# Dense layer with GELU, forward and backward: another place for the 64 left-over columns, other first loads, and a regrouped turn from block 0 to block 1

## The chip, the core and the metric

The kernel runs on one core of a Trainium2 chip, in one launch. The metric is the device time of that launch in microseconds (us). The core has five engines that run side by side and meet through semaphores: TensorE (PE in the profile, with its weight loads as PEld), VectorE (DVE), ScalarE (ACT), GpSimd (POOL) and SyncE (SP), which only issues DMAs here. ACT and POOL can issue DMAs too; all DMAs share 16 DMA engines.

## What is computed

```python
# x: 2048 x 448, w1: 448 x 1792, w2: 1792 x 448, b1: 1792, b2: 448; all bf16
h   = gelu(x @ w1 + b1)        # tanh form of GELU
out = h @ w2 + b2
# returned: out, and for a given grad_out the gradients of x, w1, b1, w2, b2
```

With u = x @ w1 + b1 and gh = (grad_out @ w2^T) * gelu'(u), the gradients are gx = gh @ w1^T, gw1 = x^T @ gh, gb1 = the column sums of gh, gw2 = h^T @ grad_out and gb2 = the column sums of grad_out.

## The kernel before

**Sizes.** The inner dimension of 448 is three tiles of 128 (`KF` = 3) and 64 left-over columns (`DL` = 64). The 2048 rows are cut into four blocks of 512 (`NB`, `SB`). The 1792 hidden columns are 14 tiles, taken in seven pairs (`NPAIR`). A step `g` is one pair of one block, so there are 28 steps; block 0 is steps 0 to 6.

**One step.** For the pair, PE makes u with w1 as weights (`M1`, L226, three products of 512 columns for each half, six in all) and q = grad_out @ w2^T (`M4`, L245, six products). The 64 left-over columns of both are done by `rest`: one product of u uses the lower 64 rows of the array (L236) and one of q the upper 64 rows (L239), and the two run side by side. To make that fit, x lies so that its left-over columns are in partitions 0 to 63 of the fourth tile and grad_out has its own in partitions 64 to 127. ACT then adds the bias and copies u to V (`act_first`, L252, two), squares it (L253), takes the GELU (L254), and in `act_second` a tanh (L272). DVE forms the derivative: `dve_first` (Bt, L269), `dve_second` (p, then t+1, p-0.5 and their product: L276, L277, L278, L279) and `dve_gate`, which multiplies with q out of PSUM into ghT (L282).

**Products of the blocks.** A `Unit` is one row tile of `out` ("o") or `gx` ("g"): 14 products of 448 columns (L313), one for each hidden tile, spread over the steps by `seq` and `grow`. In block 0 each step does eight of them (four "o" units, two products each), which need the two w2 tiles of that step. A finished unit is moved out of PSUM by ACT (L327) or DVE (L329) in `flush`, and stored by POOL (L333).

**Buffers that tie the order.** q has one PSUM buffer, so `rest(g+1, g)` of the next step waits for `dve_gate` of the step before. u has one PSUM buffer, so `M1(g+2)` waits for ACT's two copies of `act_first(g+1)`. V, A and Bt have one buffer each.

**Order of a step.** The loop at the end of the main function writes the order out by hand: `rest(g+1, g)`, `M4(g)`, DVE's evictions, `dve_gate(g)`, `act_first(g+1)`, ACT's evictions, `dve_first(g+1)`, `act_second(g+1)`, `dve_second(g+1)`, the products of the units, `M1(g+2)`. In step 6 the products come ahead of `act_second`; in step 7 the first four products come ahead of `M1(9)` and the rest behind it.

**The start.** SP issues, one behind the other: x of block 0 as two transposing DMAs (three tiles, L139, then one tile, L140), grad_out as two (L144, L145), w2^T for the first pair as two (L155, L156), then w2, w1 and w2^T in pieces (L152, L148/L149, L155/L156), x and grad_out of block 1, and w1^T. ACT issues b1 (L171) and w1 columns 0 to 255; POOL clears six tiles of `gh_nat` (L168) and then issues w1 columns 256 to 511. PE starts with seven products of zeros (L180), the 14 one-column products that turn b1 into a column (L184), and three more products of zeros (L187). Before `M4(0)` it does four products whose result nobody reads (L384). I call all of these awake-products.

**The end.** After step 27, "o" and "g" units of the last block are finished, then gw1 (L471, L479) and gw2 (L490) are made from all rows.

Of the kernel before, what the change touches and what calls it, by code (L numbers as in the profile page):

```python
# [18 lines left out]
def kernel(  # L19
# [15 lines left out]
    nc = tc.nc  # L35
    P = 128
    B, S, D = x.shape
# [3 lines left out]
    NF = F // P  # L41
    KD = (D + P - 1) // P
    KF = KD - 1
    DL = D - KF * P
    DOV = D - P
    DM = KF * P
    SB = 512
    NB = S // SB
    SPB = SB // P
    NPAIR = NF // 2  # L50
# [3 lines left out]
    x2 = x.rearrange("b s d -> (b s) d")  # L54
# [26 lines left out]
    gh_nat = const.tile([P, NB, NF, SB], BF16, name="gh_nat")  # L81
# [7 lines left out]
    w1_sb = w1_flat.rearrange("p (k f) -> p k f", k=KD)  # L89
# [9 lines left out]
    def xq(b):  # L99
        o = (b % 2) * 2 * KD * SB  # L100
        return xg_flat[:, o:o + KD * SB].rearrange("p (k s) -> p k s", k=KD)

    def gq(b):
        o = ((b % 2) * 2 + 1) * KD * SB
        return xg_flat[:, o:o + KD * SB].rearrange("p (k s) -> p k s", k=KD)

    def ring(t, n, g):
        o = (g % n) * 2 * SB
        return t[:, o:o + 2 * SB].rearrange("p (h s) -> p h s", h=2)

    def hT(g):
        return ring(hT_flat, HR, g)

    def ghT(g):
        return ring(ghT_flat, GR, g)

    def V_of(g):
        return VA_flat[:, 0:2 * SB].rearrange("p (h s) -> p h s", h=2)

    def A_of(g):  # L120
        return VA_flat[:, 2 * SB:4 * SB].rearrange("p (h s) -> p h s", h=2)

    def B_of(g):
        return ring(B_flat, 1, g)

    def t_of(g):
        return ring(T_flat, 4, 2 * (g % 2))

    def p_of(g):
        return ring(T_flat, 4, 2 * (g % 2) + 1)  # L130
# [5 lines left out]

    def load_x(b):
        rows = slice(b * SB, (b + 1) * SB)
        nc.sync.dma_start_transpose(out=xq(b)[:, 0:KF, :], in_=x2[rows, DL:D])  # L139
        nc.sync.dma_start_transpose(out=xq(b)[:, KF, :], in_=x2[rows, 0:P])  # L140

    def load_g(b):
        rows = slice(b * SB, (b + 1) * SB)
# [1 line left out]
        nc.sync.dma_start_transpose(out=gq(b)[:, 0:KF, :], in_=g2[rows, 0:DM])  # L145

    def load_w1(eng, f0, f1):
        eng.dma_start(out=w1_sb[:, 0:KF, f0:f1], in_=w1[DL:D, f0:f1].rearrange("(k p) f -> p k f", p=P))  # L148
        eng.dma_start(out=w1_sb[0:DL, KF, f0:f1], in_=w1[0:DL, f0:f1])  # L149

    def load_w2(eng, t0, t1):
        eng.dma_start(out=w2_sb[:, t0:t1, :], in_=w2[t0 * P:t1 * P, :].rearrange("(t p) d -> p t d", p=P))  # L152

    def load_w2T(f0, f1):
        nc.sync.dma_start_transpose(out=w2T_sb[:, KF, f0:f1], in_=w2[f0:f1, DOV:D])  # L155
        nc.sync.dma_start_transpose(out=w2T_sb[:, 0:KF, f0:f1], in_=w2[f0:f1, 0:DM])  # L156
# [6 lines left out]
    b1_row = T_flat[0:1, 4 * SB:4 * SB + F]  # L163
# [1 line left out]
    nc.vector.memset(ones, 1.0)  # L165
    nc.vector.memset(w128[:], 1.0 / P)

    nc.gpsimd.memset(gh_nat[:, NB - 1, 0:6, :], 0.0)  # L168
    load_w1(nc.gpsimd, 256, 512)
    load_x(0)  # L170
    nc.scalar.dma_start(out=b1_row, in_=b1.rearrange("(o f) -> o f", o=1))  # L171
    load_w1(nc.scalar, 0, 256)
    nc.scalar.activation(out=T_flat[0:1, SB + 2:SB + 3], in_=ones, func=ACT.Gelu_apprx_tanh)
    load_g(0)
# [1 line left out]
    load_w2(nc.sync, 0, 2)  # L176
    load_w1(nc.sync, 512, 768)
    pw = psum_a.tile([P, SB], F32, name="acc")
    for i in range(7):
        nc.tensor.matmul(pw[:], lhsT=warm[:, 0:P], rhs=warm, start=True, stop=True)  # L180

    pb = psum_a.tile([P, SB], F32, name="acc")
# [3 lines left out]
    for i in range(3):  # L186
        nc.tensor.matmul(pw[:], lhsT=warm[:, 0:P], rhs=warm, start=True, stop=True)  # L187
    load_w2T(256, 512)
    load_w2(nc.sync, 2, 4)
    load_w1(nc.sync, 768, 1280)  # L190
    load_w2T(512, 768)
    load_w2(nc.sync, 4, 8)
    load_w2T(768, 1024)
    load_w1(nc.sync, 1280, F)
    load_w2T(1024, 1280)
    load_w2(nc.sync, 8, NF)
    load_w2T(1280, 1536)
    load_x(1)
    load_w2T(1536, F)
# [8 lines left out]
    def blk(g):  # L208
        return divmod(g, NPAIR)

    def cols(g, h):
        c = g % NPAIR
        return slice((2 * c + h) * P, (2 * c + h + 1) * P)
# [4 lines left out]
    def M1(g):  # L218
        if g == 0:
            u_of[g] = [psum_a.tile([P, SB], F32, name="acc")[:] for h in range(2)]  # L220
        else:
            u = psum_u.tile([P, 2, SB], F32, name="u")
            u_of[g] = [u[:, h, :] for h in range(2)]
        for h in range(2):
            for kt in range(KF):
                nc.tensor.matmul(u_of[g][h], lhsT=w1_sb[:, kt, cols(g, h)], rhs=xq(g // NPAIR)[:, kt, :],  # L226
                                 start=(kt == 0), stop=False, skip_group_check=True)
# [14 lines left out]
    def M4(g):  # L242
        for h in range(2):
            for kt in range(KF):
                nc.tensor.matmul(g_of[g][:, h, :], lhsT=w2T_sb[:, kt, cols(g, h)], rhs=gq(g // NPAIR)[:, kt, :],  # L245
                                 start=False, stop=(kt == KF - 1), skip_group_check=True)

    def act_first(g):
        u = u_of.pop(g)
        for h in range(2):  # L250
            ft = 2 * (g % NPAIR) + h
            nc.scalar.activation(out=V_of(g)[:, h, :], in_=u[h], func=ACT.Identity, bias=b1_col[:, ft:ft + 1])  # L252
        nc.scalar.activation(out=A_of(g), in_=V_of(g), func=ACT.Square, scale=math.sqrt(3.0 * GELU_C * GELU_A))  # L253
        nc.scalar.activation(out=hT(g), in_=V_of(g), func=ACT.Gelu_apprx_tanh)  # L254

# [12 lines left out]
    def dve_first(g):  # L268
        nc.vector.scalar_tensor_tensor(out=B_of(g), in0=A_of(g), scalar=3.0 * GELU_C, in1=V_of(g), op0=ALU.add, op1=ALU.mult)  # L269

    def act_second(g):
        nc.scalar.activation(out=t_of(g), in_=B_of(g), func=ACT.Tanh, scale=-1.0 / 3.0)  # L272


    def dve_second(g):
        nc.vector.scalar_tensor_tensor(out=p_of(g), in0=A_of(g), scalar=GELU_C, in1=hT(g), op0=ALU.add, op1=ALU.mult)  # L276
        nc.vector.tensor_scalar(out=t_of(g), in0=t_of(g), scalar1=1.0, scalar2=None, op0=ALU.add)  # L277
        nc.vector.tensor_scalar(out=p_of(g), in0=p_of(g), scalar1=-0.5, scalar2=None, op0=ALU.add)  # L278
        nc.vector.tensor_tensor(out=t_of(g), in0=t_of(g), in1=p_of(g), op=ALU.mult)  # L279

    def dve_gate(g):
        nc.vector.scalar_tensor_tensor(out=ghT(g), in0=t_of(g), scalar=1.0, in1=g_of.pop(g)[:], op0=ALU.add, op1=ALU.mult)  # L282

    def store_h(g):
        b, c = blk(g)
        nc.gpsimd.dma_start(out=hT_dram_v[:, 2 * c:2 * c + 2, b * SB:(b + 1) * SB], in_=hT(g))  # L286
# [50 lines left out]
    def run_pieces(units):  # L337
        for un in units:
            if un.piece():
                full.append(un)  # L340

    def flush(by_act=None):
        for un in [un for un in full if by_act in (None, un.by_act)]:
            full.remove(un)
            evict(un)
# [22 lines left out]
    rest(0, None)  # L368
    first_step(0)
    act_second(0)  # L370
    dve_second(0)
    M1(1)
    for g in range(NSTEP):
        b, c = blk(g)
        pieces = [U[k] for k in seq[b] for _ in range(NF)]
        n = len(pieces)
        own = pieces[n * c // NPAIR:n * (c + 1) // NPAIR]
        grown = [U[k] for k in grow[b] for _ in range(2)]
        nxt = g + 1 if g + 1 < NSTEP else None
        rest(nxt, g)  # L380
        if g == 0:

            for i in range(4):
                nc.tensor.matmul(pw[:], lhsT=w1_sb[:, 0, 0:P], rhs=xq(0)[:, 0, :], start=True, stop=True)  # L384
        M4(g)
        flush(False)
        dve_gate(g)
        if nxt is not None:
            act_first(nxt)
        flush(True)  # L390
        if nxt is not None:
            dve_first(nxt)
        last = b == 0 and c == NPAIR - 1
        if last:
            run_pieces(grown + own)
            flush(True)
        if nxt is not None:
            act_second(nxt)
            dve_second(nxt)
        if g == NPAIR:  # L400
            run_pieces(grown)
            M1(g + 2)
            run_pieces(own)
        elif not last:
            run_pieces(grown + own)
        if g != NPAIR and g + 2 < NSTEP:
            M1(g + 2)
        for _ in range(2):
            if g >= NPAIR - 1 and stored < g:
                store_h(stored)  # L410
                stored += 1
        if c == 2 and 0 < b < NB - 1:
            load_x(b + 1)
            load_g(b + 1)
        for t in turns.get(g, []):
            turn_gh(*t)
# [45 lines left out]
    for t0, t1 in ((0, 4), (4, HT)):  # L462
        n = (t1 - t0) * P
        for h in range(2):
            a0, a1 = t0 + h * HT, t1 + h * HT
            cs = slice(a0 * P, a1 * P)
            for kt in range(KF):
                ps = psum_a.tile([P, SB], F32, name="acc")
                psv = ps[:, 0:n].rearrange("p (t f) -> p t f", f=P)
                for st in range(NS):  # L470
                    nc.tensor.matmul(psv, lhsT=x_all[:, st, kt * P:(kt + 1) * P], rhs=gh_rows(st, a0, a1),  # L471
                                     start=(st == 0), stop=(st == NS - 1))
# [3 lines left out]
        for st in range(NS):  # L476
            for h in range(2):
                psv = ps[h * DL:(h + 1) * DL, 0:n].rearrange("p (t f) -> p t f", f=P)
                nc.tensor.matmul(psv, lhsT=x_all[:, st, KF * P:D], rhs=gh_rows(st, t0 + h * HT, t1 + h * HT),  # L479
                                 start=(st == 0), stop=(st == NS - 1), tile_position=(0, h * DL), skip_group_check=True)  # L480
        nc.scalar.copy(out=gw1_rem[:, t0 * P:t1 * P], in_=ps[:, 0:n])
        for h in range(2):
            nc.scalar.dma_start(out=out_2[KF * P:D, (t0 + h * HT) * P:(t1 + h * HT) * P],
                                in_=gw1_rem[h * DL:(h + 1) * DL, t0 * P:t1 * P])
# [45 lines left out]
```

## Time and profile before

| what | value |
|---|---|
| time of three runs | 275.56, 275.80, 275.88 us; median 275.8 us |
| the profiled execution, its own time | 275.59 us |
| its span, first to last instruction | 273.8 us |
| block 0, first `rest` of step 0 to first of step 7 | 10.46 to 45.34 us |
| blocks 1 to 3 (steps 7 to 27) | 45.34 to about 161 us |
| last units, gw1, gw2 | about 161 to 271 us |

The time of a run is a little longer than the span, which leaves out what lies before the first and after the last instruction. Times inside the profile count from the start of the span. A line of the timeline has the start, the length, the engine, the line of the kernel and the operation; in brackets stands how long the engine had been idle before it and what ended the wait. A letter q behind an engine's name marks its sequencer; DMA issues stand there, and their length is the time of the issue, not of the transfer.

### The profile page before, as it was taken

What the parts mean: (1) busy time and instruction counts of PE and PEld (TensorE: products, weight loads), DVE (VectorE), ACT (ScalarE), POOL (GpSimd) and SP (SyncE); (2) the same over time, 40 slices, a digit from 0 to 9 for tenths busy, and PEclk for the clock granted to TensorE, in tenths of its full rate; (3) what the DMA queues carried; (4) which work ended last, traced back from release to release, by engine and by line L of the source; (5) the groups of instructions that cost most, each with busy time, mean ns of one, the idle gap of its engine ahead of it and who ended that gap; (6) DMA issues with size and microseconds to landing.
All of it is one profiled execution on the core that took longest, in us unless ns stands there. A gap on an engine that the chain in (4) does not pass through costs nothing.

```text
span 273.8 us, 3596 instructions
## 1 busy us (share of the span) xinstructions
PE 267.6 (98%) x1406; PEld 123.7 (45%) x1406; DVE 189.3 (69%) x218; ACT 143.7 (52%) x188; POOL 54.6 (20%) x57
## 2 busy tenths in 40 slices
PE   7899999999999999999999999999999999999995
PEld 3343434443444344444444445554445655555552
DVE  0799999999999999999888871139999970000000
ACT  2878879788888778887777740011111221112111
POOL 6000002730301403033031135111700019400000
PEclk9999999999999999999999999999999999999999
DMA  7878979999999928055534339999999931101111
GB/s 164 172 190 193 213 117 170 274 317 246 199 242 203 249 58 163 24 154 122 138 113 79 110 105 217 325 335 241 165 201 273 225 100 57 44 9 50 50 51 35
DMA packets 101379, 43.78 MB, mean 160 GB/s; under 512 B 90353, under 2 KB 97905, under 8 KB 101362
## 3 DMA queue, kind: packets, MB, share of 16 engines
q1 hardware_dynamic: 94272, 26.68, 51.6%
q0 software_dynamic: 4544, 14.92, 16.9%
q10 hardware_dynamic: 2546, 1.95, 2.5%
q8 instruction: 11, 0.18, 0.3%
q14 instruction: 6, 0.05, 0.1%
HBM read 7.00 MB, written 14.23 MB: 78 GB/s over the span
## 4 chain that ended last, share of the span: by engine, by line
PE 82%; DVE 12%; ACT 2%; DMA 2%; issue 1%; DVEq 0%
PE acc L313 27%; PE acc L490 16%; PE acc L471 13%; PE q L245 10%; PE u L226 9%; PE u L236 4%; DVE Bt L269 3%; DVE T L276 3%; DVE ghT_h L282 3%; PE acc L479 2%; DMA xg_h<-in_x_dram 2%; DVE T L279 2%; DVE T L277 1%; DVE T L278 1%; ACT VA L252 1%
## 5 line engine op out<-in xcount | busy, mean ns | idle before, releaser
L313 PE MATMUL acc<-w_gw,hT_h 128*128 128x448 bf16 x224 | 46.3, 352 | 0.2 <-ACT VA L252 0.2
L313 PE MATMUL acc<-w1T_gw,ghT_h 128*128 128x448 bf16 x224 | 45.1, 352 | 0.0
L245 PE MATMUL q<-xg_h,w2T_g 128*128 128x512 bf16 x168 | 41.1, 381 | 0.0
L252 ACT ACTIVATE VA<-u,b_col 128x512 f32<-128x512 f32 x54 | 34.0, 679 | 13.5 <-PE u L236 12.9
L226 PE MATMUL u<-xg_h,w_x 128*128 128x512 bf16 x162 | 39.4, 379 | 0.8 <-DMA w_x<-in_w_dram 0.4
L282 DVE SCALAR_TENSOR_TENSOR ghT_h<-T,q 128x1024 bf16<-128x1024 bf16 x28 | 34.2, 1221 | 8.4 <-PE q L245 7.0
L272 ACT ACTIVATE T<-Bt 128x1024 bf16<-128x1024 f32 x28 | 29.6, 1056 | 13.9 <-DVE Bt L269 13.8
L471 PE MATMUL acc<-gh_nat,w_x 128*128 128x512 bf16 (+1 forms) x192 | 36.7, 353 | 0.0
L276 DVE SCALAR_TENSOR_TENSOR T<-VA,hT_h 128x1024 bf16<-128x1024 f32 x28 | 34.1, 1219 | 0.2 <-ACT hT_h L266 0.2
L269 DVE SCALAR_TENSOR_TENSOR Bt<-VA 128x1024 f32<-128x1024 f32 x27 | 32.9, 1219 | 0.0
L313 PEld LDWEIGHTS <-hT_h 128*128 128x128 bf16 x224 | 21.9, 98 | 22.0 <-issue 0.5
L313 PEld LDWEIGHTS <-ghT_h 128*128 128x128 bf16 x224 | 21.9, 98 | 20.9
L456 DVE TENSOR_TENSOR VA<-VA,gh_nat 128x1792 f32<-128x1792 f32 x14 | 30.0, 2142 | 0.5
L253 ACT ACTIVATE VA<-VA 128x1024 f32<-128x1024 f32 x27 | 28.5, 1057 | 0.9
L254 ACT ACTIVATE hT_h<-VA 128x1024 bf16<-128x1024 f32 x27 | 28.1, 1040 | 0.0
L471 PEld LDWEIGHTS <-w_x 128*128 128x128 bf16 x192 | 18.7, 98 | 17.8 <-issue 0.4
L245 PEld LDWEIGHTS <-w2T_g 128*128 128x128 bf16 x168 | 14.2, 97 | 24.9 <-issue 11.4
L226 PEld LDWEIGHTS <-w_x 128*128 128x128 bf16 x168 | 16.3, 98 | 20.0 <-DMA w_x<-in_w_dram 1.4
L492 ACT CAST w_gw<-acc 128x448 bf16<-128x448 f32 x13 | 6.9, 532 | 32.6 <-PE acc L490 32.6
L333 POOL DMA_DIRECT2D out_dram<-io_o x8 | 5.8, 727 | 90.3 <-DVE io_o L329 48.6
L473 ACT CAST w1T_gw<-acc 128x512 bf16<-128x512 f32 (+1 forms) x12 | 6.3, 532 | 30.1 <-PE acc L471 24.2
L286 POOL DMA_DIRECT2D hT_dram<-hT_h x28 | 20.3, 728 | 1.9 <-DMA out_dram<-io_o 1.9
(60 smaller groups left out, 234.6 us busy)
## 6 DMA issues: line engine op xcount, KB each, us to landing
hT_dram<-hT_h POOLq DMA_DIRECT2D x28, 256.0 KB, 4.5
out_dram<-io_o POOLq DMA_DIRECT2D x8, 224.0 KB, 5.0
out_dram<-io_g POOLq DMA_DIRECT2D x8, 224.0 KB, 3.6
w_x<-in_x_dram POOLq DMA_DIRECT2D x1, 1792.0 KB, 10.8
w2T_g<-in_grad_out_dram POOLq DMA_DIRECT2D x1, 1792.0 KB, 14.7
out_dram<-w_gw SPq DMA_DIRECT2D x4, 336.0 KB, 2.4
w_x<-in_w_dram SPq DMA_DIRECT2D x2, 384.0 KB, 4.0
out_dram<-w1T_gw ACTq DMA_DIRECT2D x2, 384.0 KB, 5.4
```

What stands on the lines that cost most here:

```text
L226: nc.tensor.matmul(u_of[g][h], lhsT=w1_sb[:, kt, cols(g, h)], rhs=xq(g // NPAIR)[:, kt, :], start=(kt == 0), stop=False, skip_group_check= ...
L245: nc.tensor.matmul(g_of[g][:, h, :], lhsT=w2T_sb[:, kt, cols(g, h)], rhs=gq(g // NPAIR)[:, kt, :], start=False, stop=(kt == KF - 1), skip_ ...
L252: nc.scalar.activation(out=V_of(g)[:, h, :], in_=u[h], func=ACT.Identity, bias=b1_col[:, ft:ft + 1])
L253: nc.scalar.activation(out=A_of(g), in_=V_of(g), func=ACT.Square, scale=math.sqrt(3.0 * GELU_C * GELU_A))
L269: nc.vector.scalar_tensor_tensor(out=B_of(g), in0=A_of(g), scalar=3.0 * GELU_C, in1=V_of(g), op0=ALU.add, op1=ALU.mult)
L272: nc.scalar.activation(out=t_of(g), in_=B_of(g), func=ACT.Tanh, scale=-1.0 / 3.0)
L276: nc.vector.scalar_tensor_tensor(out=p_of(g), in0=A_of(g), scalar=GELU_C, in1=hT(g), op0=ALU.add, op1=ALU.mult)
L282: nc.vector.scalar_tensor_tensor(out=ghT(g), in0=t_of(g), scalar=1.0, in1=g_of.pop(g)[:], op0=ALU.add, op1=ALU.mult)
L313: nc.tensor.matmul(self.ps[:, 0:D], lhsT=lhsT, rhs=rhs, start=(ft == 0), stop=(ft == NF - 1 and not bias))
L456: nc.vector.tensor_tensor(out=gsb_v, in0=gsb_v, in1=gh_rows(st, 0, NF), op=ALU.add)
L471: nc.tensor.matmul(psv, lhsT=x_all[:, st, kt * P:(kt + 1) * P], rhs=gh_rows(st, a0, a1), start=(st == 0), stop=(st == NS - 1))
L490: nc.tensor.matmul(ps[:, 0:D], lhsT=h_blk[ft][:, st, :], rhs=g_all[:, st, :], start=(st == 0), stop=(st == NS - 1))
```

## The change

- x and w1 are cut the other way round: columns 0 to 383 are the three whole tiles and columns 384 to 447 are the left-over ones.
- x of block 0 is loaded by two transposes of two tiles each; blocks 1 and 2 by one transpose of four tiles each. The fourth tile reads 64 columns past the row's end, which are the first columns of the next row. Block 3, whose last row has no next row, is loaded by two transposes as before, and GpSimd copies the left-over 64 partitions down.
- b1 is issued by GpSimd, ahead of its memset, which clears four tiles and not six.
- w2 comes in pieces of 2, 4 and 8 tiles and not of 2, 2, 4 and 6; the last one is issued earlier in the queue.
- PE does six awake-products at first and not seven; the four in step 0 become three, ahead of the loop.
- In step 7, ACT's copies of u of step 8 come first, then the tanh of step 7 (which was in step 6); DVE does p, then its evictions, then the rest of the derivative and the gate.

```diff
     def load_x(b):
         rows = slice(b * SB, (b + 1) * SB)
-        nc.sync.dma_start_transpose(out=xq(b)[:, 0:KF, :], in_=x2[rows, DL:D])
-        nc.sync.dma_start_transpose(out=xq(b)[:, KF, :], in_=x2[rows, 0:P])
+        if b < NB - 1:
+            src = x2[rows, 0:D]
+            for k0, k1 in ((0, 2), (2, KD)) if b == 0 else ((0, KD),):
+                nc.sync.dma_start_transpose(
+                    out=xq(b)[:, k0:k1, :],
+                    in_=bass.AP(src.tensor, src.offset + k0 * P, [src.ap[0], [1, (k1 - k0) * P]]))
+        else:
+            nc.sync.dma_start_transpose(out=xq(b)[:, KF, :], in_=x2[rows, DOV:D])
+            nc.sync.dma_start_transpose(out=xq(b)[:, 0:KF, :], in_=x2[rows, 0:DM])
+            nc.gpsimd.tensor_copy(out=xq(b)[0:DL, KF, :], in_=xq(b)[DL:P, KF, :])
...
-        eng.dma_start(out=w1_sb[:, 0:KF, f0:f1], in_=w1[DL:D, f0:f1].rearrange("(k p) f -> p k f", p=P))
-        eng.dma_start(out=w1_sb[0:DL, KF, f0:f1], in_=w1[0:DL, f0:f1])
+        eng.dma_start(out=w1_sb[:, 0:KF, f0:f1], in_=w1[0:DM, f0:f1].rearrange("(k p) f -> p k f", p=P))
+        eng.dma_start(out=w1_sb[0:DL, KF, f0:f1], in_=w1[DM:D, f0:f1])
...
-    nc.gpsimd.memset(gh_nat[:, NB - 1, 0:6, :], 0.0)
+    nc.gpsimd.dma_start(out=b1_row, in_=b1.rearrange("(o f) -> o f", o=1))
+    nc.gpsimd.memset(gh_nat[:, NB - 1, 0:4, :], 0.0)
     load_w1(nc.gpsimd, 256, 512)
     load_x(0)
-    nc.scalar.dma_start(out=b1_row, in_=b1.rearrange("(o f) -> o f", o=1))
     load_w1(nc.scalar, 0, 256)
...
-    for i in range(7):
+    for i in range(6):
         nc.tensor.matmul(pw[:], lhsT=warm[:, 0:P], rhs=warm, start=True, stop=True)
...
     load_w2T(256, 512)
-    load_w2(nc.sync, 2, 4)
+    load_w2(nc.sync, 2, 6)
     load_w1(nc.sync, 768, 1280)
     load_w2T(512, 768)
-    load_w2(nc.sync, 4, 8)
     load_w2T(768, 1024)
+    load_w2(nc.sync, 6, NF)
     load_w1(nc.sync, 1280, F)
     load_w2T(1024, 1280)
-    load_w2(nc.sync, 8, NF)
     load_w2T(1280, 1536)
...
     M1(1)
+    for i in range(3):
+        nc.tensor.matmul(pw[:], lhsT=w1_sb[:, 0, 0:P], rhs=xq(0)[:, 0, :], start=True, stop=True)
     for g in range(NSTEP):
...
         rest(nxt, g)
-        if g == 0:
-            for i in range(4):
-                nc.tensor.matmul(pw[:], lhsT=w1_sb[:, 0, 0:P], rhs=xq(0)[:, 0, :], start=True, stop=True)
         M4(g)
-        flush(False)
-        dve_gate(g)
-        if nxt is not None:
-            act_first(nxt)
+        if g == NPAIR:
+            act_copy(nxt)
+            act_second(g)
+            dve_p(g)
+            flush(False)
+            dve_rest(g)
+            dve_gate(g)
+            act_rest(nxt)
+        else:
+            flush(False)
+            dve_gate(g)
+            if nxt is not None:
+                act_copy(nxt)
+                act_rest(nxt)
         flush(True)
         if nxt is not None:
             dve_first(nxt)
...
             flush(True)
-        if nxt is not None:
+        elif nxt is not None:
             act_second(nxt)
-            dve_second(nxt)
+            dve_p(nxt)
+            dve_rest(nxt)
```

`act_copy` and `act_rest` are the two halves of `act_first` (the copies of u; the square and the GELU), `dve_p` and `dve_rest` those of `dve_second` (p alone; the other three).

## The prediction

> **What bounds the kernel now.** First the busy shares and the summary of the chain that ended last, both on the page:
>
> ```profile
> PE 267.6 (98%) x1406; PEld 123.7 (45%) x1406; DVE 189.3 (69%) x218; ACT 143.7 (52%) x188; POOL 54.6 (20%) x57
> PE 82%; DVE 12%; ACT 2%; DMA 2%; issue 1%; DVEq 0%
> ```
>
> PE is almost always busy, but a share averages over stages. So next the chain in order of time (start, length, what):
>
> ```profile
> 0.73 4.96 DMA xg_h<-in_x_dram
> ...
> 5.73 1.46 PE acc L226 x6
> ...
> 13.46 1.05 ACT hT_h L254
> 14.51 1.22 DVE Bt L269
> ...
> 18.44 1.22 DVE ghT_h L282
> 19.66 1.13 DVE Bt L269
> ...
> 47.73 0.69 ACT VA L252
> 48.42 0.04 issue
> 48.46 1.45 PE u L226 x6
> ```
>
> Three stages. Until 14.5 us: the load of x, then a chain through PE and ACT. From 14.5 to 47.7 us DVE: a step takes 5.07 us (gates at 13.37, 18.44, 23.51 in the timeline). From 48.5 us PE, without a gap, to the last eviction at 270.6. The change leaves the products of the third stage as they are, so what it is worth is **how much earlier or later PE's unbroken work begins**, near 51 us. I follow two terms: when gate(0) runs (it starts DVE's cadence), and the turn at steps 6 to 8.
>
> **Term 1, the start.** The timeline from 4 to 14 us:
>
> ```profile
> 4.24 0.50 PE L184 MATMUL acc<-T 1*128 1x1 bf16 x14
> 4.67 0.82 PE L187 MATMUL acc<-T 128*128 128x512 bf16 x3
> 5.73 1.46 PE L226 MATMUL acc<-xg_h,w_x 128*128 128x512 bf16 x6 [0.24 <-DMA xg_h<-in_x_dram]
> 7.12 0.60 PE L236 MATMUL acc<-xg_h,w_x 64*128 64x512 bf16 x2
> 11.00 1.04 PE L384 MATMUL acc<-xg_h,w_x 128*128 128x512 bf16 x4
> 11.87 1.46 PE L245 MATMUL q<-xg_h,w2T_g 128*128 128x512 bf16 x6
> 12.32 0.69 DVE L279 TENSOR_TENSOR T<-T 128x1024 bf16<-128x1024 bf16 x1
> 13.37 1.22 DVE L282 SCALAR_TENSOR_TENSOR ghT_h<-T,q 128x1024 bf16<-128x1024 bf16 x1 [0.35 <-PE q L245]
> ```
>
> *Four awake-products leave step 0.* They start 0.215 apart, so M4(0) began 0.87 late, and gate(0) waited for it. Without them gate(0) follows its own chain: L279 ends at 13.01, and in later steps the gate starts 0.10 behind (18.34 to 18.44): 13.11 and not 13.37, **-0.26**. M4(0) also needs its w2T, issued at 8.17, whose landing is not in the trace; transposes of that shape land 3.0 to 3.5 after issue (median row 3.5), so 11.2 to 11.7, and M4(0) ends at 12.7 to 13.2. That just suffices. The three new awake-products (0.65) stand behind M1(1), which ends near 9.6; PE waits there for w2T until 10.46 anyway (0.55 idle), so they cost nothing; without that cover, up to 0.65.
>
> *x by two and two tiles.* Before, M1(0) needed only the first transpose (three tiles, 0.73 + 4.96 = 5.69). Now its third product needs the second one. Both together still move four tiles. In the DMA view the 16 engines are 99% busy from 2 to 4 us and over 100% to 6 us, so the last byte comes when it came before: the second transpose, issued at 2.15, landed 4.2 later, 6.35. Bounds: 5.69, if it comes as early as the three tiles did, and 7.3, if it takes as long as grad_out's second one (issued 4.74, 5.1 later). I take 6.35. M1(0) then does two products early and waits; its third starts at 6.39, three more follow 0.215 apart to 7.03, and L236 starts 0.31 behind: 7.34 and not 7.12, **+0.22**. From L236 to L279 all is one chain (ACT copy 7.54, squares 8.26, GELU 9.32, p 10.39), so all of it shifts.
>
> *Others at the start, at nothing.* w1 0:256 on ACT goes 0.55 sooner without b1 ahead (issue of b1 0.52); PE then waits for x, not for w1. One awake-product fewer (0.43 each, started 0.43 apart) is covered by the wait for x. POOL: b1's issue (rows 0.51 to 0.94) and 4/6 of the 2.66 us memset (1.77) together end at 3.0 to 3.4, where w1 256:512 is issued now (3.33).
>
> *b1 through POOL.* POOL's small stores took 3.2 (3.5 KB) and 4.3 us (0.9 KB), its two w1 loads 4.8 and 4.1; from 0.73 that is 3.9 to 5.5. The nearest row is 3.2, same size, with quiet DMA engines, and they are idle until 2 us: 3.9. Until 4.8 it costs nothing (0.43 for L184, 0.65 for L187, two products of 0.215, all before 6.35). The Trainium skill ("DMA: Bandwidth & Descriptors", section "Specifications") puts the first byte at about 1 us on GpSimd's path and 0.6 on ACT's; b1 would be 0.4 later by that, an estimate; no run shows both paths with b1. It would land under 4.7 and the sum would stay.
>
> Term 1: -0.26 + 0.22 = **-0.04**.
>
> **Term 2, the turn.** The timeline of steps 6 to 8:
>
> ```profile
> 46.20 1.06 ACT L272 ACTIVATE T<-Bt 128x1024 bf16<-128x1024 f32 x1
> 47.16 1.25 ACT L252 ACTIVATE VA<-u,b_col 128x512 f32<-128x512 f32 x2
> 48.46 1.45 PE L226 MATMUL u<-xg_h,w_x 128*128 128x512 bf16 x6 [0.36 <-ACT VA L252]
> 48.88 1.15 DVE L329 TENSOR_TENSOR io_o<-acc,b_bc 128x448 bf16<-128x448 f32 x2
> 49.95 1.21 DVE L282 SCALAR_TENSOR_TENSOR ghT_h<-T,q 128x1024 bf16<-128x1024 bf16 x1
> 51.36 0.39 PE L236 MATMUL u<-xg_h,w_x 64*128 64x512 bf16 x1
> ```
>
> ACT's copies of u(8) now run at 46.20 ahead of the tanh, end at 47.45, and M1(9) no longer waits: the 0.36 idle goes. But what is late next is `rest(9,8)`, which needs the q buffer, so gate(7). DVE is full there (Bt 44.94, p 46.08, three small ones, two evictions, gate 49.95). In the new order p and the evictions run to 48.4, while the tanh runs 47.48 to 48.54. Then t+1 at 48.57, and by the spacings of step 2 (0.34, 0.46, 0.79) the gate at 50.16, ending at 51.38. PE stands at `rest(9,8)` by 51.0 and waits: 51.43 and not 51.36, **+0.07**. Bounds: if DVE closes up, gate(7) stays at 49.95 and PE starts at 51.2, -0.15; if the tanh comes half a copy later (0.3), +0.4. After that PE has about 0.5 to spare on gate(8) (56.27 against 56.87).
>
> **Loads in block 0.** Landing times by size:
>
> ```profile
> w_gw<-in_w_dram SPq DMA_DIRECT2D x1, 672.0 KB, 5.5
> w_gw<-in_w_dram SPq DMA_DIRECT2D x2, 224.0 KB, 3.0
> w_gw<-in_w_dram SPq DMA_DIRECT2D x1, 448.0 KB, 4.9
> ```
>
> w2 tiles 2 to 5 (448 KB, issued near 13.9) land at 17.6 to 18.8; step 1's products stand at 17.9. A delay of up to 0.9 is taken by the slack between M4(2)'s end (22.8) and gate(2) (23.51). w2 tiles 6 to 13 (896 KB, issued near 20.7 behind the two w2T): by the line from 224 to 672 KB 6.8 us, so 27.5, and step 3's products stand at 27.8. Cost nothing, with little cover; the price is a rival below.
>
> **Later parts, at nothing.** x(1) as one transpose saves an SP issue of 1.26; x is needed at 38.8, landed at 35.2. GpSimd's copy of 64x512: between 0.44 (512/3072 of the memset) and 4.6 (its 128x448 all-reduce); I take 0.5. POOL idles 92 to 103 us, x(3) landed near 82, its reader is `rest(21,20)` at 117.4; even 4.6 fits.
>
> **Sum:** 275.59 - 0.04 + 0.07 = 275.62 against the profiled execution's own 275.59. That one lies 0.2 under the median of the three, 275.8, so I forecast **275.8 us, no change**. What this kernel's runs can tell apart is about 0.2%, 0.55 us.
>
> **Rivals.**
> 1. *The second half of x comes early* (5.69). For: w1 no longer queues behind b1. Against: the DMA engines are full. M1(0) would gain 0.43 and not lose 0.22, gate(0) then hangs on M4(0) at 12.75 at best: -0.62, with -0.11 from the turn about -0.7: 275.1.
> 2. *PE's clock stays low through M1(0).* The first products start 0.43 apart, those from 4.67 on 0.215: the clock rose near 4.2, after 3 us of unbroken products. Now there are six, and then a pause if b1 is late, and one near 5.7. If M1(0) runs at 0.43, the products from 6.39 on end 0.87 later, and DVE's whole cadence with them: 276.7. Decided by whether b1's products follow at once. For: less work before the rise. Against: 3.9 for b1 leaves no pause before 4.2. The Trainium skill ("TensorE: Matmul & The Clock Gate", Part 1) has a free-running window of about 3.4 us that must have been busy; missed once, it would lift the clock at about 7.6, an estimate, and cost 0.6. The rise in this trace fits such a window.
> 3. *The long w2 load is late.* At the slowest row (448 KB in 3.1 us behind the load ahead, 19.9 to 23.0) 896 KB end at 28.2 and w1's last 512 columns (448 KB) at 31.3, where M1(5) stands at 29.3: 2.0 late, less the 0.93 between M4(4)'s end (32.73) and gate(4) (33.66): +1.05. Half of that or more: 276.3 to 276.9, say 276.6.
> 4. *b1 lands at 5.5*: M1(0) starts at 6.65, L236 0.7 later than in my sum: 276.5.
>
> **Chances.** Forecast 0.52, rival 1 0.18, rival 2 0.14, rival 3 0.11, rival 4 0.05. Within 0.2% lie the forecast and the milder part of rival 3 (0.03): same 0.55; faster is rival 1, 0.18; slower is the rest, 0.14 + 0.08 + 0.05 = 0.27. The forecast's own range, from the bounds of the two terms (-0.15 and +0.4 of the turn, about ±0.3 of x), is 275.3 to 276.4; the range that holds 8 in 10 reaches to rivals 1 and 2: 275.1 to 276.7.
>
> **What would show it.** Right: M1(0)'s third product at about 6.4, behind the second x transpose; gate(0) at 13.3; no idle before M1(9); a wait of 0.3 to 0.5 before L239 of step 8, ended by gate(7), at 51.4. Wrong: gate(0) under 12.9 (rival 1), L226 0.43 apart (rival 2), L313 of step 3 or M1(5) waiting for a DMA (rival 3), L184 after 5 us (rival 4), or any new gap in PE after 52 us.

## The result and the profile after

The changed kernel takes 278.22 us (median of six, 277.61 to 278.91) against 275.68 us; the ratio on record is 1.0086, 95% interval 1.0072 to 1.0101 (the two medians alone give 1.0092). It is slower by 0.9%, outside the forecast range of 275.1 to 276.7. The profiled execution took 278.26 us with a span of 276.5 us. The changed kernel has other line numbers: L190 are the awake-products at the start, L194 b1's products, L197 the three products of zeros, L235 `M1`, L245 and L248 `rest`, L254 `M4`, L295 `dve_gate`, L326 the units.

The page of the changed kernel, busy shares and summary of the chain:

```profile
PE 269.4 (97%) x1390; PEld 124.2 (45%) x1404; DVE 189.1 (68%) x218; ACT 143.6 (52%) x188; POOL 54.8 (20%) x59
PE 81%; DVE 12%; ACT 3%; DMA 1%; issue 1%; DVEq 0%; POOLq 0%
```

The shares hardly moved; 2.5 us cannot be seen in them. The chain in order of time shows where they are:

```profile
1.29 3.81 DMA T<-in_b_dram
5.09 0.05 issue
5.14 0.53 PE acc L194 x14
5.67 1.39 PE acc L197 x3
7.06 2.56 PE acc L235 x6
9.62 0.55 PE acc L245
```

Before, the chain began with the load of x and had M1(0)'s six products at 1.46 us. Now it begins with **the load of b1**, and the same six products take 2.56 us. The timeline of the start shows why:

```profile
1.18 2.74 PE L190 MATMUL acc<-T 128*128 128x512 bf16 x6 [1.18 <-DVE T L175]
...
1.29 0.63 POOL L178 DMA_DIRECT2D T<-in_b_dram  x1 [0.85 <-POOLq L539]
...
5.14 0.53 PE L194 MATMUL acc<-T 1*128 1x1 bf16 x14 [1.22 <-DMA T<-in_b_dram]
5.60 1.46 PE L197 MATMUL acc<-T 128*128 128x512 bf16 x3
...
6.85 2.77 PE L235 MATMUL acc<-xg_h,w_x 128*128 128x512 bf16 x6
...
9.55 1.03 PE L245 MATMUL acc<-xg_h,w_x 64*128 64x512 bf16 x2
...
15.77 1.22 DVE L295 SCALAR_TENSOR_TENSOR ghT_h<-T,q 128x1024 bf16<-128x1024 bf16 x1
```

GpSimd issues b1 at 1.29, not at 0.73, and it lands at 5.1. PE has done its six awake-products by 3.9 and stands idle for 1.22 us. That is the only time in the whole trace that PE waits for a DMA. After the pause everything runs 0.43 apart, M1(0) and `rest(0)` included, up to 10.5 us, where the spacing falls to 0.22. `rest(0)` begins at 9.55 and not at 7.12 (+2.43), gate(0) at 15.77 and not at 13.37 (+2.40). The turn, later:

```profile
50.11 1.46 PE L235 MATMUL u<-xg_h,w_x 128*128 128x512 bf16 x6
...
52.52 1.22 DVE L295 SCALAR_TENSOR_TENSOR ghT_h<-T,q 128x1024 bf16<-128x1024 bf16 x1
...
53.80 0.37 PE L248 MATMUL q<-xg_h,w2T_g 64*128 64x512 bf16 x1 [0.40 <-DVE ghT_h L295]
```

q of step 8 begins at 53.80 and not at 51.36: +2.44, so nothing was lost or won between gate(0) and here but 0.04. PE's last product ends at 273.02 and not at 270.60 (+2.42). The two profiled executions differ by 2.67 us in all; the other 0.25 lies outside PE's work.

### The profile page after: what moved, and what is told of

Same layout as the page of the kernel before. It is cut to its first block, busy times and chain, and to the rows that moved or that the text cites. A ratio compares the mean times of both kernels' runs of the same rounds, so it can differ in the third digit from the quotient of the medians.

```text
span 276.5 us, 3577 instructions
## 1 busy us (share of the span) xinstructions
PE 269.4 (97%) x1390; PEld 124.2 (45%) x1404; DVE 189.1 (68%) x218; ACT 143.6 (52%) x188; POOL 54.8 (20%) x59
## 4 chain that ended last, share of the span: by engine, by line
PE 81%; DVE 12%; ACT 3%; DMA 1%; issue 1%; DVEq 0%; POOLq 0%
PE acc L326 26%; PE acc L515 15%; PE acc L496 13%; PE q L254 10%; PE u L235 8%; PE u L245 3%; DVE T L287 3%; DVE ghT_h L295 3%; DVE Bt L280 2%; PE acc L504 2%; DVE T L292 2%; DMA T<-in_b_dram 1%; DVE T L290 1%; PE acc L235 1%; DVE T L291 1%
## 5 line engine op out<-in xcount | busy, mean ns | idle before, releaser
L326 PE MATMUL acc<-w_gw,hT_h 128*128 128x448 bf16 x224 | 46.3, 352 | 0.1
L326 PE MATMUL acc<-w1T_gw,ghT_h 128*128 128x448 bf16 x224 | 45.1, 352 | 0.0
L254 PE MATMUL q<-xg_h,w2T_g 128*128 128x512 bf16 x166 | 40.7, 381 | 0.2 <-issue 0.2
L295 DVE SCALAR_TENSOR_TENSOR ghT_h<-T,q 128x1024 bf16<-128x1024 bf16 x28 | 34.2, 1220 | 8.1 <-PE q L254 6.6
L235 PE MATMUL u<-xg_h,w_x 128*128 128x512 bf16 x150 | 38.8, 379 | 0.6
L326 PEld LDWEIGHTS <-hT_h 128*128 128x128 bf16 x224 | 21.9, 98 | 21.6
L326 PEld LDWEIGHTS <-ghT_h 128*128 128x128 bf16 x224 | 21.9, 98 | 20.9
L235 PEld LDWEIGHTS <-w_x 128*128 128x128 bf16 x168 | 16.7, 100 | 20.2 <-issue 2.5
L254 PEld LDWEIGHTS <-w2T_g 128*128 128x128 bf16 x168 | 14.1, 97 | 25.1 <-issue 11.8
```

The costliest lines, as they stand in the source:

```text
L326: nc.tensor.matmul(self.ps[:, 0:D], lhsT=lhsT, rhs=rhs, start=(ft == 0), stop=(ft == NF - 1 and not bias))
```

## The experiments

Theory A: b1 lands late through GpSimd, PE pauses, and the pause keeps PE's clock low. Theory B: six awake-products are too few by themselves. Theory C: the second x transpose (landing at 7.37, issued at 2.12 and 5.25 us under way) holds M1(0). All times were taken beside runs of the kernel before, whose median over all 80 of these was 275.74 us. Kernels that start from the changed one are named a_, from the kernel before b_.

**a_b1_act**

```diff
-    nc.gpsimd.dma_start(out=b1_row, in_=b1.rearrange("(o f) -> o f", o=1))
-    nc.gpsimd.memset(gh_nat[:, NB - 1, 0:4, :], 0.0)
+    nc.gpsimd.memset(gh_nat[:, NB - 1, 0:6, :], 0.0)
...
     load_x(0)
+    nc.scalar.dma_start(out=b1_row, in_=b1.rearrange("(o f) -> o f", o=1))
```

> The changed kernel with b1 issued by ACT ahead of w1 again, and GpSimd's memset back at six tiles; the six awake-products and everything else stay. Theory A (b1 lands late through GpSimd, PE pauses, and the pause keeps the clock low): b1's products start near 3.8 us, no pause, products after 4.7 us start 0.215 apart; M1(0)'s third product then waits for the second x transpose alone, 6.4 to 7.4 us; 275.6 to 276.7 us. Theory B (six awake-products are too few by themselves): M1(0) still 0.43 apart, 277.2 us or more. Theory C (the second x transpose holds M1(0)): M1(0)'s third product at 7.4 us at full clock, 276.6 us or more.

Measured: 276.65 us, ratio 1.0042 (1.0026 to 1.0058). Its timeline:

```profile
3.86 0.53 PE L194 MATMUL acc<-T 1*128 1x1 bf16 x14
4.32 1.46 PE L197 MATMUL acc<-T 128*128 128x512 bf16 x3
5.57 0.73 PE L235 MATMUL acc<-xg_h,w_x 128*128 128x512 bf16 x2
7.18 1.02 PE L235 MATMUL acc<-xg_h,w_x 128*128 128x512 bf16 x4 [0.89 <-DMA xg_h<-in_x_dram]
```

b1's products follow the awake-products without a pause, and b1 is there 1.2 us or more sooner than through GpSimd (5.09). The clock is up by 5.9. 1.57 of the 2.5 us are gone. What is left is the third product, which waits for x until 7.18: that is theory A for the larger part and C for the rest.

**a_awake9**

```diff
-    for i in range(6):
+    for i in range(9):
```

> The changed kernel with nine awake-products at the start and not six, so that they reach from 1.2 to about 5.0 us; b1 stays on GpSimd. Theory A: the clock rises near 4.2 us although b1 still lands near 5.1; M1(0) starts near 6.2 at 0.215 apart, its third product at 6.7 to 7.4 with x; 276.0 to 276.8 us, so the low clock alone was worth 1.4 to 2.2 us and b1 and x the rest. Theory B says the same. Theory C: 276.6 to 276.8, with the third product waiting for x. If M1(0) still runs 0.43 apart, pause and count of products are both not the cause.

Measured: 276.70 us, 1.0039 (1.0025 to 1.0053).

```profile
1.18 4.02 PE L190 MATMUL acc<-T 128*128 128x512 bf16 x9 [1.18 <-DVE T L175]
5.14 0.53 PE L194 MATMUL acc<-T 1*128 1x1 bf16 x14
5.60 1.46 PE L197 MATMUL acc<-T 128*128 128x512 bf16 x3
6.85 1.55 PE L235 MATMUL acc<-xg_h,w_x 128*128 128x512 bf16 x6
8.33 0.60 PE L245 MATMUL acc<-xg_h,w_x 64*128 64x512 bf16 x2
```

b1's products start at 5.14 as in the changed kernel, and M1(0) at the same 6.85, but its six products take 1.55 and not 2.77 us. The only thing filled in is the pause. So the low clock that follows the pause is worth 1.5 us (278.22 - 276.70), with b1's products as late as before. The clock rose later than I expected, between 6.85 and 7.16, not at 4.2. About 1.0 us over the kernel before is left. In this execution it is not a wait for x, whose second transpose landed at 7.14, ahead of M1(0)'s third product at 7.37; it is M1(0)'s late start, behind nine awake-products, b1's products and three more of zeros.

**b_b1_pool**

```diff
-    nc.gpsimd.memset(gh_nat[:, NB - 1, 0:6, :], 0.0)
+    nc.gpsimd.dma_start(out=b1_row, in_=b1.rearrange("(o f) -> o f", o=1))
+    nc.gpsimd.memset(gh_nat[:, NB - 1, 0:4, :], 0.0)
...
-    nc.scalar.dma_start(out=b1_row, in_=b1.rearrange("(o f) -> o f", o=1))
```

> The kernel before with b1 alone moved to GpSimd, ahead of a memset of four tiles; seven awake-products, x by three tiles and one. b1 lands near 5.1 us and PE pauses from 4.1 to 5.1. Theory A: the pause keeps the clock low, M1(0) 0.43 apart, 277.2 to 278.2 us. Theory B: seven products were enough to raise the clock at 4.2, so only b1's lateness counts, M1(0) at 6.25 and not 5.73: 276.2 us. Theory C: b1 costs little, 275.7 to 276.2.

Measured: ratio 1.0043 (1.0023 to 1.0064), but the median of 276.79 us stands between two groups: six times of 275.90 to 276.04 and six of 277.55 to 278.20, nothing between. The profiled execution (276.03) is one of the first group:

```profile
5.07 0.50 PE L184 MATMUL acc<-T 1*128 1x1 bf16 x14 [0.73 <-DMA T<-in_b_dram]
5.50 0.82 PE L187 MATMUL acc<-T 128*128 128x512 bf16 x3
6.38 1.46 PE L226 MATMUL acc<-xg_h,w_x 128*128 128x512 bf16 x6
```

Here the pause of 0.73 came after the clock had risen (L187 0.22 apart), and the executions of this group lie 0.2 to 0.3 us above the kernel before. Not all of that can be put down to b1. In the profiled execution it was x's first transpose that released M1(0), late itself (6.34, before 5.69); the chain has

```profile
0.73 5.61 DMA xg_h<-in_x_dram
6.34 0.04 issue
6.38 1.46 PE acc L226 x6
```

and behind b1's products alone M1(0) could have begun near 6.16 (L187's three products, 0.22 apart from 5.50). The second group lies 1.5 to 2.3 us higher, about the price of the low clock in a_awake9 or more; no execution of it was profiled, so its clock is inferred. The same kernel can go either way: A's numbers were hit by one half of the executions, and B's nearly (276.0 for 276.2) by the other. An explanation that is argued and not shown: the pause starts at 4.35 here, after the clock's rise in some executions and ahead of it in others. In the changed kernel it starts at 3.92, ahead of the earliest rise in any trace (near 4.0, b_x31), and all six executions took 277.61 us or more.

**b_x22** (only the new `load_x` and `load_w1`)

> The kernel before with the new cut of x and w1 alone (two and two tiles for block 0, four at once for blocks 1 and 2, GpSimd's copy for block 3); b1 on ACT, seven awake-products. Theories A and B: the clock rises near 4.2 us as before, and only the second x transpose counts: third product of M1(0) at 6.4 us (my forecast, +0.2, 275.9 us) up to 7.4 us (+1.2, 276.9). Theory C: 7.4 us, 276.9 or more.

Measured: 276.44 us, 1.0041 (1.0023 to 1.0058).

```profile
5.84 0.59 PE L236 MATMUL acc<-xg_h,w_x 128*128 128x512 bf16 x2
7.08 1.02 PE L236 MATMUL acc<-xg_h,w_x 128*128 128x512 bf16 x4 [0.65 <-DMA xg_h<-in_x_dram]
```

The wait for x is there with b1 on ACT and seven awake-products: +0.7 us from x by itself. The next two runs ask why the second transpose is late.

**b_x31**

```diff
-            for k0, k1 in ((0, 2), (2, KD)) if b == 0 else ((0, KD),):
+            for k0, k1 in ((0, KF), (KF, KD)) if b == 0 else ((0, KD),):
```

(against b_x22)

> The kernel before with the new cut of x and w1, but x of block 0 loaded by three tiles and one (the one tile still reads past the row's end). Theory S (the split into two and two holds M1(0), since the second transpose lands at 7.0 to 7.4 us): landings at 5.7 and 6.3 us, M1(0) at 5.7 without a break, gate(0) near 13.4, 275.7 us. Theory E (reading past the row's end, or the other cut, is what is slow): the one-tile transpose lands near 7.0, rest(0) waits for it, gate(0) near 13.9, 276.3 us.

Measured: 275.89 us, 1.0003 (0.9995 to 1.0012). Reading past the row's end costs nothing; the split does. This execution also showed where a good start goes. M1(0) began at 5.27 and gate(0) at 12.66, 0.71 sooner than before; then, in step 2:

```profile
22.07 1.25 PE L255 MATMUL q<-xg_h,w2T_g 128*128 128x512 bf16 x5 [1.32 <-DMA w2T_g<-in_w_dram]
...
23.57 1.22 DVE L292 SCALAR_TENSOR_TENSOR ghT_h<-T,q 128x1024 bf16<-128x1024 bf16 x1 [0.87 <-remote]
```

M4(2) waits for its w2T, and gate(2) stands at 23.57, where it stood before (23.51). All of the 0.71 was given back. That load was issued at 16.82 in both traces; the view of it at 16.9 to 17.0 us, the kernel before first, has

```profile
w2T_g<-in_w_dram SPq DMA_TRANSPOSE x1, 3.1
```

```profile
w2T_g<-in_w_dram SPq DMA_TRANSPOSE x1, 5.2
```

so it landed at 22.0 and not at 19.9. Why it took 2.1 us longer, and whether the earlier start has to do with it, is not shown.

**b_x22_w1_late**

```diff
-    nc.gpsimd.memset(gh_nat[:, NB - 1, 0:6, :], 0.0)
+    nc.gpsimd.memset(gh_nat[:, NB - 1, 0:10, :], 0.0)
```

(against b_x22)

> The new cut alone with two and two tiles, and GpSimd's memset lengthened from six to ten tiles, so that its w1 load is issued near 5.1 us and not 3.3; M1(1) will wait for it, so the time itself says little. Theory P (the 4 KB packets of GpSimd's w1 load, which run from 5.5 us on, hold the last writes of the second x transpose): the second x transpose lands near 6.3 us. Theory S: it lands at 7.0 us or later all the same.

Measured, a single execution: 275.92 us. The second x transpose, still two tiles, landed 4.2 us after its issue at 2.12, so at 6.3. The DMA view of the issues at 2.1 to 2.3 us, b_x22 first, then this kernel:

```profile
xg_h<-in_x_dram SPq DMA_TRANSPOSE x1, 4.9
```

```profile
xg_h<-in_x_dram SPq DMA_TRANSPOSE x1, 4.2
```

Theory P holds and S falls: two tiles are late only when GpSimd's w1 load meets them. What it meets inside the DMA engines is not shown, nor why one tile that meets the same load is not late (b_x31: issued at 2.16, landed at 6.04). By the packet records the last packet of x starts at 5.4 us in b_x22 and at 5.3 here. In b_x22 the 4 KB packets of w1 begin at 5.6 and take 0.57 us each on average; in the kernel before they begin at 5.9 and take 0.24 us.

**b_awake_moved**

```diff
+    for i in range(3):
+        nc.tensor.matmul(pw[:], lhsT=w1_sb[:, 0, 0:P], rhs=xq(0)[:, 0, :], start=True, stop=True)
     for g in range(NSTEP):
...
-        if g == 0:
-            for i in range(4):
-                nc.tensor.matmul(pw[:], lhsT=w1_sb[:, 0, 0:P], rhs=xq(0)[:, 0, :], start=True, stop=True)
```

> The kernel before with the four awake-products of step 0 replaced by three ahead of the loop, nothing else. My forecast's term: gate(0) at 13.11 and not 13.37, 0.26 sooner all the way to the end, 275.5 us. Rival: M4(0) then waits for its w2T (landing 11.2 to 11.7 us) and gate(0) stays at 13.3: 275.7 us.

Measured: 275.76 us, 0.9998 (0.9988 to 1.0009). The time cannot tell -0.26 from nothing. Inside its profiled execution the clock rose late (M1(0) 0.43 apart at first), but from `rest(0)` (7.71) to gate(0) (13.71) it took 6.00 us against 6.25 before: the term is there, and M4(0), which waited 0.22 us for its w2T, did not wait long enough to spoil it.

**b_turn** (only step 7's new order)

> The kernel before with step 7's new order alone. My forecast's term: no idle before M1(9), but q of step 8 waits for gate(7); PE's unbroken work starts 0.07 later, 275.8 us. Rival: gate(7) stays at 49.95 and PE gains 0.15, 275.6 us.

Measured: 275.93 us, 1.0004 (0.9991 to 1.0017). From gate(0) (13.69) to q of step 8 (51.82) 38.13 us against 37.99: no gain, as forecast, and 0.14 lost where I had 0.07.

**a_mended** (b1 on ACT with six tiles of memset, seven awake-products, x by three tiles and one; all else as changed)

> The changed kernel with three things put back: b1 on ACT (memset of six tiles), seven awake-products, and x of block 0 by three tiles and one. Kept are the new cut, the moved awake-products, w2 in three loads and step 7's order. If only b1 and the split of x made the change slower, this stands with the kernel before or below it: gate(0) near 12.7 to 13.1, 275.1 to 275.8 us. If another part costs too, it stays above 276.

Measured: 275.73 us, 1.0001 (0.9991 to 1.0012). The rest of the change is worth nothing either way. gate(0) stood at 13.32 in the profiled execution and not at 12.7 to 13.1; the clock was up only by 5.9 there.

**a_w1_late** (a_b1_act with seven awake-products and a memset of eight tiles)

> The changed kernel with b1 on ACT, seven awake-products, x still by two and two, and GpSimd's memset at eight tiles, so that its w1 load is issued near 4.2 us and not 3.3. Theory P (its packets hold the second x transpose): x lands near 6.4 and not 7.1, gate(0) near 13.4, 275.4 to 276.0 us, against 276.65 with six tiles. Theory S (two tiles at a time are late by themselves): x at 7.0 or later, 276.4 us or more.

Measured: 275.84 us, 1.0004 (0.9995 to 1.0013). x by two and two no longer costs; the second transpose took 4.0 us from 2.12. Theory P again. gate(0) stood at 13.93 and not at 13.4, since in this execution the clock rose only near 7.1:

```profile
4.74 1.46 PE L197 MATMUL acc<-T 128*128 128x512 bf16 x3
6.00 2.00 PE L235 MATMUL acc<-xg_h,w_x 128*128 128x512 bf16 x6
```

**b_w2_three** (only the three loads of w2)

> The kernel before with w2 in three loads alone. My forecast: nothing, 275.7 us; the 896 KB land near 27.5 us and step 3's products stand at 27.8. Rival 3 of the forecast: it is late and costs 0.5 to 1 us, 276.3 or more. Third case: step 2 no longer waits for w2 at 23 us and 0.1 to 0.3 us are gained.

Measured: 275.91 us, 1.0004 (0.9995 to 1.0013). Neither the loss of rival 3 nor the small gain.

**b_awake6** (only six awake-products and not seven)

> The kernel before with six awake-products at the start and not seven, b1 on ACT. Theory A: without a pause six suffice, 275.7 us, at most 0.3 more where the clock rises a little later. Theory B: some or all executions run M1(0) at half clock, 276.5 to 278 us.

Measured: 275.58 us, 0.9994 (0.9984 to 1.0003). Theory B falls: six products without a pause are enough. No version clearly below the kernel before came out of this.

## Why the prediction was wrong, point by point

**b1 through GpSimd: the failed step.** I put b1's landing at 3.9 us, from the row of 3.2 us counted from 0.73. It was issued at 1.29, because GpSimd's queue came to it 0.56 later than the other queues began, and took 3.8. My limit "until 4.8 it costs nothing" was passed by 0.3, within my upper end of 5.5. By lateness alone that cost at most 0.2 to 0.3 us (b_b1_pool's lower group).

**The clock: the mechanism was a rival, its condition was mispriced.** Rival 2 asked "whether b1's products follow at once" and had 0.14, rival 4 had b1's late landing with 0.05. They are one event: a late b1 makes the pause, and the pause keeps the clock low. I priced each without the other, and argued rival 2 away with the very landing that failed ("3.9 for b1 leaves no pause before 4.2"). The clock rose near 10.5 us, so all eight products of M1(0) and `rest(0)`, and the three of zeros ahead of them, ran at half speed, not only those from 6.39 on (0.87); my estimate of 7.6 for the rise after one missed window was 3 us too early. Putting b1 back takes off 1.57 us (a_b1_act), and filling the pause alone 1.5 (a_awake9). The two do not add up, since after either M1(0) is held by the next thing in line: by x after the one, by its late start after the other. As the sum had it, a delay here goes through DVE's cadence to the end undiminished; a gain of 0.71 did not (b_x31).

**x by two and two: mis-sized.** +0.22 had its third product at 6.39; in a kernel without the clock's trouble it came at 7.08 (b_x22), and `rest(0)` at 8.04 and not at 7.34. My argument that the last byte comes when it came before was right for x's packets and wrong for the landing: the 7.3 of the upper bound was nearer, once w1 crosses it. In the changed kernel itself this was hidden, since the third product started at 7.71 anyhow; it would have shown with b1 mended, and did (a_b1_act, +0.9 us in all).

**Awake-products of step 0: right.** From ACT's first copy to gate(0) 5.83 us before (7.54 to 13.37) and 5.58 after (10.19 to 15.77): -0.25 against -0.26. The times of b_awake_moved cannot tell it from nothing.

**The turn: right.** No idle before M1(9), a wait of 0.40 for gate(7) before q of step 8, and 0.04 later against 0.07.

**w2, x of the later blocks, GpSimd's copy: right.** 896 KB took 6.6 us against 6.8, the copy 0.60 against 0.5, and a_mended, which holds them all, stands at 1.0001.

**Rival 1** (x early, at 5.69) did not come: no run saw the second transpose before 5.9.

## What to carry over

A short load that PE waits for while it is being warmed up costs more than its lateness: here a pause of 1.2 us in the first 5 us cost 1.5 us of clock, so cover it with more idle products or bring the load by the queue that starts first. Two rivals that share a trigger are one case and have to be priced as one. A gain at the start is kept only if the loads behind it come in time for it; in b_x31 one late w2T of step 2 took all of it back.

## What the runs showed of the hardware

- **When the clock rises.** In the executions without a pause the spacing fell from 0.43 to 0.22 anywhere between about 4.0 (b_x31) and 7.1 us (a_w1_late), with the same products. With the pause of 1.22 us it was 10.5; with the one of 0.73 us (b_b1_pool) it was near 4.2 in the execution that was profiled, ahead of the pause. The Trainium skill ("TensorE: Matmul & The Clock Gate", Part 1) states a free-running window of about 3.4 us that must be busy; the spread of 3.1 us and the delay of about one window more fit that. How idle a window may be is not shown.
- **The granted clock does not show it.** The profile gives the changed kernel a granted clock of 1.00 from 4 to 10 us, where products start 0.43 apart; the spacing must be read. The trace's own clock records bear the spacing out: the first of them, at full clock, begins at 10.63 in the changed kernel, 4.14 in the kernel before and 4.21 in b_b1_pool, and the view shows 1.00 for the time ahead of it too. The window view has six products in 2 us below the rise and nine across it, at the same 1.00 (stretch, length, PE busy, granted clock, DMA share, GB/s):

```profile
6.00:8.00 2.00, 2.00 (x6) 1.00 0.67 121
...
10.00:12.00 2.00, 2.00 (x9) 1.00 0.94 217
```

- **GpSimd's path.** b1 landed at 5.09 through GpSimd (4.72 in a_awake9, 5.03 in b_b1_pool) and before 3.86 through ACT (a_b1_act). The Trainium skill ("DMA: Bandwidth & Descriptors", section "Specifications") has 0.4 us between the two paths for the first byte; the runs show 0.9 to 1.2 us or more to the landing, 0.56 of it ahead of the issue.
- **Two loads that cross.** A transpose of two tiles, issued at 2.12, landed at 7.0 to 7.4 us with GpSimd's w1 load issued at 3.3 to 3.7, and at 6.1 to 6.3 with it at 4.2 or 5.0.
